# Plain float32 scores on 64 rows and plain float32 weighted values in a fused attention and MLP kernel

## The chip, the cores and the metric

One NeuronCore of one Trainium2 chip runs the whole program. The metric is the device time of one execution in microseconds. Each version is timed several times and the median counts. Hardware profiles of single executions show what each engine did.

## What is computed

Two batches, 8 heads, 576 positions, head size 64. Rotary embedding on q and k, softmax attention, then two feed-forward layers on the 1152 tokens, all in float32:

```
q_rot, k_rot = rotate(q), rotate(k)              # x1*cos - x2*sin, x1*sin + x2*cos
scores = q_rot @ k_rot.T / sqrt(64)
attn = exp(scores - max); attn /= sum(attn) + 1e-9
x = (attn @ v)  -> 1152 x 512
x = ((x @ w_a) * (x @ w_b)) @ w_out              # 512 -> 1536 -> 512
h = x @ w_in;  out = (h * tanh(softplus(h))) @ w_out2     # 512 -> 2048 -> 512
```

## The kernel before

TensorE multiplies float32 in two ways here. A tile typed `fp32r` goes through the array in one pass, and the kernel then makes a float32 product of parts: high times high, high times low, low times high. A plain float32 matmul (the parts' tile viewed as float32 by `lo32`, line 453) needs no parts; the trace shows it as two weight loads and two passes.

The kernel handles heads in pairs: p = 0 to 3 is the first batch, 4 to 7 the second. A pair's 576 queries are cut into four chunks of 128 and a rest of 64 per head. A *unit* is one chunk of one head, or both heads' rests together; nine units make a pair, 72 the attention. `UNITS` (line 442) lists them: the four chunks of head 0, the rest, the four chunks of head 1.

- **Rotation** (`rope`, line 593; called by `next_pair`, line 969, and for the first pair at line 957). Products with the tables `cs` and a sum, on VectorE or GpSimd, whichever the planner picks. Then ScalarE copies each head's 64 rows of the result into a 128-row tile, q scaled by 0.125 with its low half below (`scalar_tensor_tensor` on VectorE), k twice, and `kl` holds k's low half (line 611).
- **Scores** (`scores`, line 662). For each unit and each half of the 576 keys two `fp32r` matmuls of 288 columns on 128 rows: (q high, q low) against (k, k), and against (`kl`, 0). VectorE takes the row maximum `m`. Tag `s` has two buffers of two PSUM banks each.
- **First batch** (`attend0`, line 712). ScalarE makes E = exp(s - m) in SBUF; TensorE transposes E in 128 x 128 blocks into PSUM (`tm`, and `tr` for the last 64 keys of two heads); ScalarE copies the high half as fp16 (`ptm`, `ptr`), VectorE subtracts for the low half. V is scaled by a power of two found from its largest magnitude (`v_max`, `v_scale`) and split into two fp16 parts `vhl` (`v_split`); `vr` is its last block. The weighted values (`weighted`, line 686) are three fp16 products per block: 15 matmuls per unit, `o`. A column of ones in V gives the sum. `finish` (line 763) divides, on GpSimd for the first batch.
- **Second batch** (`attend`, line 746). E is split in place into fp16 halves `pp` and transposed by DMA; the weighted values are fp16 too.
- **Layers.** `transpose_x` brings x to `xT`. Layer 1 of the first batch uses plain float32 matmuls (tile `l` from `x`, `w`), all other layers three `fp32r` passes. Weights arrive as 64-bit words; VectorE decodes one in three operations (`xw`, `w`). The first batch's layers 1 and 2 run interleaved with the second batch's attention; then follow the second batch's layers, and the last two layers (`hidden`, `accumulate`).

Nothing is issued when it is called. `record` (line 206) collects operations, and `order` (line 289), a list scheduler with its own table of costs (`cost`, line 264) and a priority set by `at(...)`, fixes each engine's order. `any` operations go to VectorE or GpSimd, `flex` ones to ScalarE or VectorE. `OFF` shifts a unit's steps against its nominal time.

Of the kernel before, what the change touches and what calls it, by code (L numbers as in the profile page):

```python
# [20 lines left out]
NP = H // 2  # L21
# [153 lines left out]
class Plan:  # L175
# [30 lines left out]
    def record(self, engine, method, args, kw):  # L206
        key = engine.key
        out = kw["out"] if "out" in kw else args[0]
        views = [v for v in list(args) + list(kw.values()) if isinstance(v, View)]
        deps, roots = [], []  # L210
        for v in views:
            t = v.root
            assert not t.dead, t.kw
            if t.first is not None:
                deps.append((t.first, False))
            elif t not in roots:
                roots.append(t)
                deps.append((t.pool.opened, True))
                if t.before is not None:
# [44 lines left out]
    def cost(self, key, method, out, args, kw, views):  # L264
# [147 lines left out]
VM = 4  # L412
# [11 lines left out]
V_AT = 3  # L424
# [18 lines left out]
for p in range(2 * NP):  # L443
    if p == NP - 1:
        UNITS += [(p, 0, 0), (p, 0, 1), (p, 1, 0), (p, 1, 1), (p, 0, 2), (p, 0, 3), (p, None, 0), (p, 1, 2), (p, 1, 3)]
    else:
        UNITS += [(p, 0, c) for c in range(4)] + [(p, None, 0)] + [(p, 1, c) for c in range(4)]
# [10 lines left out]
def kernel(ctx: ExitStack, tc: tile.TileContext, qk, v5, w1, w2, w34, tab, out):  # L458
# [97 lines left out]
    kl = [[a_p.tile([128, S], F32R, tag=f"kl{i}{h}", name=f"kl{i}{h}") for h in range(2)] for i in range(2)]  # L556


    qz = x_p.tile([128, 2, S + 64], F32R, tag=f"x{2 * NP - 1}", name="qz")
    qz = [qz[:, i, 0:256].rearrange("p (h c) -> p h c", h=2) for i in range(2)]  # L560
    xbd = [a_p.tile([128, 128], F32, tag=f"xbd{i}", name=f"xbd{i}") for i in range(2)]
    vhl = [(a_p if i < 2 else a0_p).tile([128, 5, 2, 130], F16, tag=f"vhl{i}", name=f"vhl{i}") for i in range(3)]
# [3 lines left out]
    vr = [a0_p.tile([128, 2, 130], F16, tag=f"vr{i}", name=f"vr{i}") for i in range(3)]  # L566
    vb = (0, 1, 2, 0, 1, 0, 1, 0)
# [12 lines left out]
    def parts_tile(p):  # L580


        t = a_p.tile([128, 4, S], F32R, tag="qk", name=f"qk{p}", bufs=2)
        qk_t[p] = [(t[:, 0, :], t[:, 1, :]), (t[:, 2, :], t[:, 3, :])]
# [7 lines left out]

    def rope(p, o, k, eng, cols=slice(0, S)):

        t, raw = qk_t[p][o], qkr_t[p, o, cols.start]
        x, y = raw[:, 0, cols], raw[:, 1, cols]
        if k == 0:
            eng.tensor_tensor(x, x, cs[:, 0, cols], op=ALU.mult)
        elif k == 1:
            eng.tensor_tensor(y, y, cs[:, 1, cols], op=ALU.mult)  # L600
        elif k == 2:
            eng.tensor_tensor(x, x, y, op=ALU.add)
        else:
            for h in range(2):
                r, q = slice(64 * h, 64 * h + 64), slice(64 - 64 * h, 128 - 64 * h)
                if k == 3:
                    act.activation(t[h][r, cols], x[r], AF.Copy, scale=1.0 if o else 0.125)
                    if o:
                        act.activation(t[h][q, cols], x[r], AF.Copy, scale=1.0)
                elif o:  # L610
                    eng.tensor_tensor(kl[p % 2][h][r, cols], x[r], lo32(t[h][r, cols]), op=ALU.subtract)
                else:
                    dve.scalar_tensor_tensor(
                        t[h][q, cols], x[r], 0.125, lo32(t[h][r, cols]), op0=ALU.mult, op1=ALU.subtract
                    )
                    if cols.stop == S:
                        act.copy(qz[p % 2][:, h, r], lo32(t[h][:, 512:576]))


# [4 lines left out]
    def v_max(p):  # L624
        if p < VM:

            of = vhl[min(p, len(vhl) - 1)].rearrange("p c h e -> p (c h) e")[:, :, 1 : D + 1]
            act.activation(of, v_t[p].rearrange("p (n d) -> p n d", d=D), AF.Abs, accum_out=v_mx[:, p : p + 1])
            return
# [15 lines left out]
    def v_split(p):  # L645
# [6 lines left out]
        if p < NP:  # L652
            pool.tensor_copy(vr[vb[p]][64:128, :, 0 : 2 * D + 1], v[64:128, 4, :, 0 : 2 * D + 1])
            return
# [6 lines left out]

    def scores(n):
# [4 lines left out]
        rest = h is None  # L667
        at(t0_ + OFF["S"])
        st = s_ps.tile([128, 2, 512], F32, tag="s", name=f"s{n}")
        for hf in range(2):  # L670
            ks = slice(HS * hf, HS * hf + HS)
            ops = []
            for i in (0, 1) if rest else (h,):
                lhsT = qz[p % 2][:, i, :] if rest else tq[i][:, 128 * c : 128 * c + 128]
                ops += [(lhsT, tk[i][:, ks]), (lhsT, kl[p % 2][i][:, ks])]
            for i, (lhsT, rhs) in enumerate(ops):
                pe.matmul(st[:, hf, :HS], lhsT=lhsT, rhs=rhs, start=(i == 0), stop=(i == len(ops) - 1))

        at(t0_ + OFF["M"])
# [6 lines left out]
    def weighted(n, chunks):  # L686
# [4 lines left out]
        if rest or c % 2 == 0:  # L691
            o_t[p] = (o2_ps if o2_ps and n % 2 else o_ps).tile([128, 512], F32, tag="o", name=f"o{n}")
        o = o_t[p]
        ops = [(x, v, lo, w) for x, l, v in chunks for lo, w in ((0, D + 1), (D + 1, D)) if x is not None]
        ops += [(x, v, 0, D + 1) for l, x, v in chunks if x is not None]
        for i, (x, v, lo, w) in enumerate(ops):
# [4 lines left out]
            else:  # L701
                base = 66 * (c % 2) + oc
# [3 lines left out]
        if rest or c % 2:  # L706
            at(t_unit(n) + OFF["N"])
            finish(p, rest, h, c // 2)
# [3 lines left out]
    def attend0(n):  # L712
# [4 lines left out]
        j = 0 if rest else c % 2  # L717
# [6 lines left out]
        def parts(x, name, bufs):  # L724
# [16 lines left out]
        for i in (0,) if rest else (0, 1):  # L741
            chunks = [(*(pt_t[i][:, q, 128 * k : 128 * k + 128] for q in (0, 1)), vhl[vb[p]][:, k]) for k in range(4)]
            chunks.append((*(pr[:, q, 128 * i : 128 * i + 128] for q in (0, 1)), vr[vb[p]]))
# [19 lines left out]
    def finish(p, rest, h, g):  # L763

        key = "r" if rest else h
# [3 lines left out]
        dve.tensor_scalar(den, oo[:, :, 0], 1e-9, v_up[:, p : p + 1], op0=ALU.add, op1=ALU.mult)  # L769
# [13 lines left out]
        part = early and g  # L783
        if (p, part) not in xn_t:
# [3 lines left out]
        c = 0 if early else 2 * g  # L788
        eng.tensor_tensor(
            xn_t[p, part][:, c : c + 2, h, :], oo, den.unsqueeze(2).to_broadcast([128, 2, D]), op=ALU.mult  # L790
        )
# [133 lines left out]
    for i in range(2):  # L925
        for h in range(2):
            pool.memset(lo32(kl[i][h]), 0.0)
    parts_tile(0)
# [13 lines left out]
    v_t[0] = load_v(0, a0_p, "v", 1)  # L942
    sp.dma_start(ident, tab[:, 2 * S : 2 * S + 192])
    pool.memset(ones, 1.0)
    for i in range(2):
        pool.memset(lo32(qz[i]), 0.0)
    for i in range(2):
        pool.memset(xbd[i], 0.0)
    for i in range(3):
        pool.memset(vhl[i][:, :, :, 0:1], 1.0)  # L950
        pool.memset(vr[i][0:64], 0.0)
# [5 lines left out]
    for o, c0, c1, t in ((1, 0, KC, 0), (0, 0, QC, 0), (1, KC, S, 0), (0, QC, S, Q_REST)):  # L957
        at(t)
        for i in range(5):
            rope(0, o, i, dve, slice(c0, c1))  # L960
    at(VP[0])
    v_max(0)
    v_scale(0, 1)
    v_split(0)
    for p in range(1, NP):
        at(VP[1])
        v_t[p] = load_v(p, w_p, "raw", 3)

    def next_pair(p):
# [5 lines left out]
        parts_tile(p)  # L975
        for o in range(2):
            at(max(t0 - LOAD_LEAD, 2))
            load_qk(p, o)
            for i in range(5):
                at(t0 + dt * (R0 + R1 * (5 * o + i) / 10))  # L980
# [4 lines left out]
    for n in range(NU):  # L985
# [10 lines left out]
        if n == V_AT:  # L996
# [187 lines left out]
```

## Time and profile before

| | us |
|---|---|
| median of three runs | 621.8 |
| lowest and highest of the three | 619.88, 626.88 |
| span of the profiled execution (first to last instruction) | 619.7 |

| engine | busy us | share of the span | instructions |
|---|---|---|---|
| TensorE, matmuls (PE) | 585.8 | 95% | 4192 |
| TensorE, weight loads (PEld) | 518.4 | 84% | 4192 |
| VectorE (DVE) | 482.5 | 78% | 937 |
| ScalarE (ACT) | 305.6 | 49% | 605 |
| GpSimd (POOL) | 112.3 | 18% | 114 |

The record does not give the profiled execution a time of its own beside its span; 619.7 is 0.2 under the lowest of the timed runs and 2.1 under the median.

How to read the rows. All calculating lines carry the line number of one helper (L394), so groups are told apart by their tiles: `s<-qk` writes tile s and reads qk. In a table by stretch the columns are the stretch, its length, then for PE, PEld, DVE, ACT and POOL the busy microseconds and the number of instructions, the granted TensorE clock as a share of 2.4 GHz, the DMA share and GB/s. In a table of groups they are engine, operation, tiles, shapes and count, then busy us and mean ns of one, then idle us just before them and what ended it. A timeline row gives the start, the time to the end of the last one of the row, the engine and what it did, and the number merged. Matmuls are pipelined: one lasts some 0.2 to 0.5 us from start to end, and the distance of starts is what it costs.

### The profile page before, as it was taken

The page shows a single profiled execution, that of the slowest core. Times are in us where ns is not written, and L with a number is a line of the kernel's source. Part 1 is how long each engine was busy: PE and PEld are TensorE (multiplying, and loading weights), DVE is VectorE, ACT ScalarE, POOL GpSimd, SP SyncE. Part 2 cuts the span into 40 slices and gives each one's busy share as a digit, 9 for nine tenths or more (in the row PEclk, how much of TensorE's full clock was granted, in tenths as well). Part 3 has the DMA queues.
Part 4 walks back from the last instruction along what each step waited for, and adds up shares of the span by engine and source line. Part 5 has one row for each costly group of instructions (what it writes and reads, how often), then busy time and mean ns, then how long its engine had stood idle before and what let it go on. Part 6 is the DMA issues. An engine that isn't in the chain of part 4 may idle for free.

```text
span 619.7 us, 10977 instructions
## 1 busy us (share of the span) xinstructions
PE 585.8 (95%) x4192; PEld 518.4 (84%) x4192; DVE 482.5 (78%) x937; ACT 305.6 (49%) x605; POOL 112.3 (18%) x114
## 2 busy tenths in 40 slices
PE   5788888989989999999999999999999999999997
PEld 5677787867768778999999999997888899988985
DVE  6999998999999899896999999859989334332221
ACT  4889697556447455551444443245444344342320
POOL 5366683735152001110000000000000000000000
PEclk7799897999999999999999999999999999999999
DMA  8024131978879699799665575657887124220002
GB/s 303 2 77 128 53 116 66 264 178 205 215 181 194 151 204 211 148 184 360 214 194 183 186 228 202 237 170 259 303 285 255 52 70 153 84 68 1 1 0 86
DMA packets 78916, 100.25 MB, mean 162 GB/s; under 512 B 50832, under 2 KB 52496, under 8 KB 78864
## 3 DMA queue, kind: packets, MB, share of 16 engines
q1 hardware_dynamic: 78864, 99.55, 55.9%
q8 instruction: 33, 0.54, 0.4%
q14 instruction: 19, 0.16, 0.1%
HBM read 77.50 MB, written 10.75 MB: 142 GB/s over the span
## 4 chain that ended last, share of the span: by engine, by line
PE 71%; DVE 17%; ACT 8%; issue 2%; DMA 1%; SPq 0%; ACTq 0%; DVEq 0%
PE l L394 32%; PE acc L394 16%; PE h L394 15%; PE s L394 3%; DVE xw L394 3%; PE o L394 3%; DVE m L394 2%; ACT qk L394 2%; DVE qk L394 2%; DVE w L394 2%; DVE ptm L394 1%; ACT e L394 1%; DVE pp L394 1%; ACT ptm L394 1%; PE tm L394 1%
## 5 line engine op out<-in xcount | busy, mean ns | idle before, releaser
L394 PE MATMUL l<-x,w 128*128 128x256 f32 (+1 forms) x960 | 180.9, 343 | 0.3
L394 PEld LDWEIGHTS l<-x,w 128*128 128x128 f32 x960 | 146.1, 190 | 16.2 <-DVE ab L394 0.8
L394 DVE SCALAR_TENSOR_TENSOR xw<-wr,xw 128x512 uint32<-128x512 uint32 x184 | 131.0, 725 | 1.3
L394 PE MATMUL acc<-w,g 128*128 128x512 f32 x432 | 105.7, 396 | 0.0
L394 PE MATMUL h<-y,w 128*128 128x320 f32 (+1 forms) x576 | 104.8, 336 | 0.3 <-DVE g L394 0.3
L394 PEld LDWEIGHTS h<-y,w 128*128 128x128 f32 x576 | 93.5, 188 | 9.7 <-DVE g L394 0.7
L394 PEld LDWEIGHTS acc<-w,g 128*128 128x128 f32 x432 | 80.6, 188 | 18.5 <-ACT g L394 0.5
L394 PE MATMUL l<-ab,w 128*128 128x320 f32 (+1 forms) x576 | 79.6, 297 | 0.0
L394 PEld LDWEIGHTS l<-ab,w 128*128 128x128 f32 x576 | 77.2, 190 | 0.0
L394 DVE TENSOR_TENSOR w<-wc,w 128x512 fp32r<-128x512 f32 x39 | 26.8, 691 | 56.2 <-ACT w L394 54.8
L394 ACT CAST w<-xw 128x512 fp32r<-128x512 f32 x73 | 45.2, 622 | 43.6 <-DVE xw L394 23.1
L394 DVE TENSOR_REDUCE m<-s 128x1 f32<-128x576 f32 x72 | 53.1, 747 | 2.5 <-PE s L394 2.1
L394 ACT ACTIVATE h<-h 128x320 f32<-128x320 f32 (+1 forms) x48 | 22.8, 475 | 58.5 <-PE h L394 58.4
L394 DVE TENSOR_SCALAR xw<-wr 128x512 uint32<-128x512 uint32 x104 | 48.9, 484 | 2.9 <-DMA wr<-in_w_dram 2.4
L394 PE MATMUL s<-qk 128*128 128x288 f32 x128 | 44.3, 361 | 6.0 <-DVE qk L394 3.1
L394 DVE TENSOR_TENSOR w<-xw,w 128x512 fp32r<-128x512 f32 x66 | 45.0, 684 | 5.5 <-ACT w L394 5.3
L394 POOL TENSOR_TENSOR qkr<-qkr,cs 128x576 f32<-128x576 f32 x28 | 43.8, 1578 | 29.8 <-DMA qkr<-in_qk_dram 25.4
L394 DVE TENSOR_TENSOR g<-h,g 128x320 fp32r<-128x320 f32 (+1 forms) x48 | 26.6, 554 | 28.3 <-ACT g L394 28.3
L394 ACT CAST w<-wc 128x512 fp32r<-128x512 f32 x39 | 23.9, 617 | 38.0 <-PE acc L394 33.7
L394 ACT ACTIVATE s<-s,m 128x576 f32<-128x576 f32 x36 | 25.4, 713 | 30.8 <-DVE m L394 27.8
L394 PE MATMUL s<-kl,qk 128*128 128x288 f32 x128 | 38.1, 311 | 2.0 <-DVE kl L394 2.0
L394 PEld LDWEIGHTS s<-qk 128*128 128x128 f32 x128 | 25.3, 199 | 10.3 <-ACT e L394 4.4
(96 smaller groups left out, 753.9 us busy)
## 6 DMA issues: line engine op xcount, KB each, us to landing
wr<-in_w_dram SPq DMA_DIRECT2D x104, 512.0 KB, 4.2
wc<-kc SPq DMA_DIRECT2D x39, 256.0 KB, 2.7
kc<-xw SPq DMA_DIRECT2D x32, 256.0 KB, 2.7
qkr<-in_qk_dram SPq DMA_DIRECT2D x14, 576.0 KB, 4.9
v<-in_v_dram SPq DMA_DIRECT2D x8, 320.0 KB, 6.5
out_dram<-o_sb SPq DMA_DIRECT2D x9, 256.0 KB, 2.1
pt<-pp SPq DMA_TRANSPOSE x36, 3.7
vh<-vhl SPq DMA_DIRECT2D x8, 66.0 KB, 2.8
```

The lines of the kernel that those rows point to most:

```text
L394: getattr(engine, method)(*map(real, args), **{k: real(v) for k, v in kw.items()})
```

## The change

Three things. First, scores of both batches become plain float32: q and k keep one float32 tile per pair (`rotated`), 64 rows per head, with no halves; the factor 0.125 moves into a second set of tables `cq` for q that ScalarE makes once; `kl` and the copies by ScalarE are gone. A head's scores are one plain matmul on its 64 rows per half of the keys, head 0 on rows 0 to 63, head 1 on rows 64 to 127. The two heads of a chunk are computed together, alternating, into both score tiles, so the units are listed by chunk and not by head. The rest is a plain matmul on 128 rows. Second, in the first batch the transposed E is copied once, as float32, by ScalarE or VectorE (`flex`), and multiplied with V as float32 (`v32`), which the DMA puts into place beside the column of ones; V's scaling, splitting, `vr` and the low halves are gone there. A unit has 5 plain matmuls in place of 15 fp16 ones. Third, the planner's cost for plain matmuls changes. The second batch's weighted values stay as they are.

```diff
@@ record
-        for v in views:
+        for v in views + list(also):
...
@@ cost
+            if rhs.dtype == F32 and method == "matmul":
+                n = max(n, 560 if views[1].n == 128 else 0)
+            if rhs.a.shape[0] == 64 and rhs.dtype == F32:
+                n /= 2
...
@@ UNITS
-        UNITS += [(p, 0, c) for c in range(4)] + [(p, None, 0)] + [(p, 1, c) for c in range(4)]
+        chunks = (0, 1, None, 2, 3)
+    for c in chunks:
+        UNITS += [(p, None, 0)] if c is None else [(p, 0, c), (p, 1, c)]
...
+    def load_v32(p):
+        b, c = divmod(p, NP)
+        src = v5[b, c]
+        sp.dma_start(v32[p][:, 0:4, :, 1 : D + 1], src[:, 0:4])
+        sp.dma_start(v32[p][64:128, 4, :, 1 : D + 1], src[64:128, 4])
...
@@ rope
         elif k == 2:
-            eng.tensor_tensor(x, x, y, op=ALU.add)
-        else:
+            eng.tensor_tensor(t[:, cols], x, y, op=ALU.add)
+        elif not o and cols.stop == S:
             for h in range(2):
-                r, q = slice(64 * h, 64 * h + 64), slice(64 - 64 * h, 128 - 64 * h)
-                if k == 3:
-                    act.activation(t[h][r, cols], x[r], AF.Copy, scale=1.0 if o else 0.125)
-                    if o:
-                        act.activation(t[h][q, cols], x[r], AF.Copy, scale=1.0)
-                elif o:
-                    eng.tensor_tensor(kl[p % 2][h][r, cols], x[r], lo32(t[h][r, cols]), op=ALU.subtract)
...
+                r = slice(64 * h, 64 * h + 64)
+                act.copy(qz[p % 2][r, r], t[r, 512:576])
...
@@ scores
+        if not h:
+            at(t0_ + OFF["S"])
+            heads = (0,) if h is None else (0, 1)
+            for i in heads:
+                s_t[i] = s_ps.tile([128, 2, 512], F32, tag="s", name=f"s{n + i}")
+            for hf in range(2):
+                ks = slice(HS * hf, HS * hf + HS)
+                for i in heads:
+                    r = slice(0, 128) if h is None else slice(64 * i, 64 * i + 64)
+                    lhsT = qz[p % 2] if h is None else tq[r, 128 * c : 128 * c + 128]
+                    also = [s_t[1]] if h == hf == i == 0 else []
+                    pe.matmul(s_t[i][:, hf, :HS], lhsT=lhsT, rhs=tk[r, ks], start=True, stop=True, also=also)
...
@@ weighted
+        if p < NP:
+            ops = [(x, v, 0, D + 1) for x, v in chunks]
...
@@ attend0
-            pt = a0_p.tile([128, 2, w], F16, tag=f"p{name}", name=f"p{name}{n}", bufs=6)
-            act.copy(pt[:, 0, :], t)
-            dve.tensor_tensor(pt[:, 1, :], t, pt[:, 0, :], op=ALU.subtract)
+            pt = a0_p.tile([128, w], F32, tag=f"p{name}", name=f"p{name}{n}", bufs=6)
+            flex.copy(pt, t, scale=1.0)
...
@@ start
+        if not o:
+            act.activation(cq[:, :, c0:c1], cs[:, :, c0:c1], AF.Copy, scale=0.125)
-        for i in range(5):
+        for i in range(4):
             rope(0, o, i, dve, slice(c0, c1))
-    at(VP[0])
-    v_max(0)
-    v_scale(0, 1)
-    v_split(0)
...
```

The planner moves the work. At the start of the program, VectorE's order of before, up to the first maximum (`m`):

```order
1 L394 TENSOR_TENSOR qkr_k<-qkr_k,cs 128x320 x2
2 L394 TENSOR_TENSOR qkr_q<-qkr_q,cs 128x256
3 L394 TENSOR_TENSOR qkr_k<-qkr_k 128x320
4 L394 TENSOR_TENSOR qkr_q<-qkr_q,cs 128x256
5 L394 TENSOR_TENSOR qkr_q<-qkr_q 128x256
6 L394 TENSOR_TENSOR kl_88<-qkr_k,qk_169 64x320
...
13 L394 TENSOR_TENSOR kl_88<-qkr_k,qk_169 64x256
14 L394 TENSOR_TENSOR qkr_q<-qkr_q 128x320
15 L394 TENSOR_TENSOR kl_95<-qkr_k,qk_169 64x256
16 L394 TENSOR_REDUCE m_218<-s_192 128x1
```

And now:

```order
1 L399 TENSOR_TENSOR qkr_k<-qkr_k,cs 128x320 x2
2 L399 TENSOR_TENSOR qkr_q<-qkr_q,cq 128x256
3 L399 TENSOR_TENSOR qk_159<-qkr_k 128x320
4 L399 TENSOR_TENSOR qkr_q<-qkr_q,cq 128x256
5 L399 TENSOR_TENSOR qk_159<-qkr_q 128x256
6 L399 TENSOR_TENSOR qkr_k<-qkr_k,cs 128x256 x2
7 L399 TENSOR_TENSOR qk_159<-qkr_k 128x256
8 L399 TENSOR_TENSOR qkr_q<-qkr_q,cq 128x320 x2
9 L399 TENSOR_REDUCE m_191<-s_178 128x1
```

The four subtractions `kl` and the low halves of q are no longer there, and the products of q read `cq`.

In the middle of the first batch, TensorE's order of before holds, between the transposes `tm` and the fp16 weighted values `o` (each with its load), two units' scores from the parts in `qk` and `kl`:

```order
937 L394 MATMUL tm_1384<-ident,e_1364 128x128 x2
938 L394 MATMUL s_1389<-qk_1059 128x288
939 L394 MATMUL s_1389<-kl_108,qk_1059 128x288
940 L394 MATMUL s_1389<-qk_1059 128x288
941 L394 MATMUL s_1389<-kl_108,qk_1059 128x288
942 L394 MATMUL tm_1384<-ident,e_1364 128x128 x2
943 L394 MATMUL s_1401<-qk_1059 128x288
944 L394 MATMUL s_1401<-kl_108,qk_1059 128x288
945 L394 MATMUL s_1401<-qk_1059 128x288
946 L394 MATMUL s_1401<-kl_108,qk_1059 128x288
947 L394 LDWEIGHTS ptm_1332
948 L394 MATMUL o_1410<-vhl_143,ptm_1332 128x65
```

Now, at the same place (`s_970` is head 0, `s_971` head 1 of one chunk):

```order
160 L399 MATMUL s_970<-qk_565 128x288
161 L399 MATMUL s_971<-qk_565 128x288
162 L399 MATMUL s_970<-qk_565 128x288
163 L399 MATMUL s_971<-qk_565 128x288
164 L399 MATMUL tm_950<-ident,e_861 128x128
165 L399 MATMUL tr_979<-ident,e_861 128x128 x2
166 L399 MATMUL o_960<-v_105,ptm_916 128x65 x4
167 L399 MATMUL o_960<-v_105,ptr_921 128x65
168 L399 MATMUL tm_999<-ident,e_923 128x128 x4
169 L399 MATMUL tm_1010<-ident,e_923 128x128 x2
170 L399 MATMUL o_1015<-v_105,ptm_958 128x65 x4
171 L399 MATMUL o_1015<-v_105,ptr_990 128x65
```

The scores of a chunk stand together with the heads alternating, and ten transposes and ten weighted values stand between one chunk's scores and the next. On VectorE the same place now reads, between the maxima of two chunks, with decoding of layer-1 weights (`xw`) where subtractions stood:

```order
100 L399 TENSOR_REDUCE m_985<-s_970 128x1
101 L399 TENSOR_REDUCE m_994<-s_971 128x1
102 L399 TENSOR_SCALAR den_0_2_1003<-o_960 128x2
103 L399 TENSOR_SCALAR xw_1006<-wr_934 128x512
104 L399 RECIPROCAL den_0_2_1003<-den_0_2_1003 128x2
105 L399 TENSOR_SCALAR ptm_1017<-tm_999 128x512
106 L399 SCALAR_TENSOR_TENSOR xw_1006<-wr_934,xw_1006 128x512
107 L399 TENSOR_SCALAR xw_1031<-wr_988 128x512
108 L399 TENSOR_REDUCE m_1035<-s_1025 128x1
```

Nine of these weights are begun, and six of them finished, ahead of the first layer-1 result. In all TensorE's order has 2240 rows where it had 3430.

## Rows read from the trace of the kernel before

**Rows 1.** Table by stretch: first batch alone, interleaved (two rows), layers of second batch.
```profile
16.00:110.00 94.00, 78.02 (x900) 69.57 (x901) 88.02 (x177) 77.68 (x161) 55.06 (x56) 0.91 0.24 75
110.00:200.00 90.00, 83.26 (x574) 65.00 (x571) 88.04 (x170) 50.40 (x95) 37.47 (x26) 1.00 0.87 207
200.00:284.00 84.00, 83.89 (x709) 73.11 (x707) 77.69 (x167) 40.50 (x75) 9.41 (x7) 1.00 0.84 189
284.00:414.00 130.00, 130.00 (x972) 129.91 (x972) 115.86 (x231) 47.84 (x102) 1.42 (x4) 1.00 0.65 221
```
**Rows 2.** Groups of instructions from 16 to 110 us, VectorE and ScalarE.
```profile
L394 DVE TENSOR_REDUCE m<-s 128x1 f32<-128x576 f32 x36 | 26.6, 746 | 1.7 <-PE s L394 1.6
L394 ACT ACTIVATE e<-s,m 128x576 f32<-128x576 f32 x36 | 26.4, 744 | 5.9 <-DVE m L394 5.6
...
L394 DVE TENSOR_TENSOR ptm<-tm,ptm 128x512 f16<-128x512 f32 x36 | 24.3, 680 | 1.8 <-ACT ptm L394 1.5
...
L394 DVE SCALAR_TENSOR_TENSOR qk<-qkr,qk 64x576 fp32r<-64x576 f32 x8 | 7.8, 975 | 0.3
L394 DVE TENSOR_TENSOR ptr<-tr,ptr 128x256 f16<-128x256 f32 x16 | 6.5, 409 | 0.1
...
L394 DVE SCALAR_TENSOR_TENSOR vhl<-v,v_up,vhl 128x640 f16<-128x640 f32 x5 | 5.5, 1096 | 0.0
...
L394 DVE SCALAR_TENSOR_TENSOR xw<-wr,xw 128x512 uint32<-128x512 uint32 x4 | 3.4, 850 | 0.0
```
**Rows 3.** Chain of waits that ends last, its beginning: start us, us, what.
```profile
2.77 5.13 DMA qkr_k<-in_qk_dram
...
13.17 1.53 DVE kl L394
...
15.13 1.52 DVE kl L394
...
16.69 0.77 DVE m L394
```
**Rows 4.** Timeline of TensorE's matmuls from 61.3 to 62.4 us.
```profile
61.38 0.41 PE L394 MATMUL o<-vhl,ptm 128*128 128x65 f16 x8
61.63 0.23 PE L394 MATMUL o<-vr,ptr 128*128 128x65 f16 x2
...
61.76 0.38 PE L394 MATMUL s<-qk 128*128 128x288 f32 x1
61.97 0.30 PE L394 MATMUL s<-kl,qk 128*128 128x288 f32 x1
62.10 0.29 PE L394 MATMUL s<-qk 128*128 128x288 f32 x1
```
**Rows 5.** The same from 152 to 154.2 us: plain float32 matmuls of layer 1.
```profile
152.31 1.89 PE L394 MATMUL l<-x,w 128*128 128x256 f32 x8
154.04 0.35 PE L394 MATMUL o<-vhl,pt 128*128 128x65 f16 x6
```
**Rows 6.** Timeline of TensorE's weight loads from 85.0 to 85.8 us.
```profile
85.27 0.30 PEld L394 LDWEIGHTS xt<-ident,xbd 128*128 128x128 f32 x2
85.43 0.26 PEld L394 LDWEIGHTS tm<-ident,e 128*128 128x128 f32 x2
```
**Rows 7.** Timelines of TensorE, matmuls and weight loads, from 145.9 to 147 us.
```profile
145.67 0.81 PE L394 MATMUL l<-x,w 128*128 128x256 f32 x3
...
146.72 0.48 PE L394 MATMUL l<-x,w 128*128 128x256 f32 x1
...
146.41 0.29 PEld L394 LDWEIGHTS vs<-vm,ones 1*128 1x128 f32 x2 [0.33 <-DVE vm L394]
146.71 0.30 PEld L394 LDWEIGHTS l<-x,w 128*128 128x128 f32 x2
```
**Rows 8.** Timeline from 109.9 to 111 us: the first matmul of layer 1.
```profile
110.19 1.11 PE L394 MATMUL l<-x,w 128*128 128x256 f32 x4
```

More of the change, by code (lines that the diff above doesn't have):

```diff
@@ L218, in record @@
                 deps.append((t.pool.opened, True))
-                if t.before is not None:
+                if t.before is not None and t.before not in roots:
                     deps.append((t.before.first, False))
@@ L410 @@
 HOLD = 40
-VM = 4
 KC = 320
@@ L666, in scores @@
         tq, tk = qk_t[p]
[L667 to L677, printed above, removed]
+        if not h:
[10 more added lines that the diff above has]
+                    pe.matmul(s_t[i][:, hf, :HS], lhsT=lhsT, rhs=tk[r, ks], start=True, stop=True, also=also)
+        st = s_t[h or 0]
         at(t0_ + OFF["M"])
@@ L690, in weighted @@
         at(t_unit(n) + OFF["V"])
-        if rest or c % 2 == 0:
+        if not h:
             o_t[p] = (o2_ps if o2_ps and n % 2 else o_ps).tile([128, 512], F32, tag="o", name=f"o{n}")
         o = o_t[p]
-        ops = [(x, v, lo, w) for x, l, v in chunks for lo, w in ((0, D + 1), (D + 1, D)) if x is not None]
-        ops += [(x, v, 0, D + 1) for l, x, v in chunks if x is not None]
+        if p < NP:
+            ops = [(x, v, 0, D + 1) for x, v in chunks]
+        else:
+            ops = [(x, v, lo, w) for x, l, v in chunks for lo, w in ((0, D + 1), (D + 1, D)) if x is not None]
+            ops += [(x, v, 0, D + 1) for l, x, v in chunks if x is not None]
         for i, (x, v, lo, w) in enumerate(ops):
@@ L716, in attend0 @@
         t0_ = t_unit(n)
-        j = 0 if rest else c % 2
+        j = h or 0
         s, m = scores(n)
@@ L741, in attend0 @@
         for i in (0,) if rest else (0, 1):
-            chunks = [(*(pt_t[i][:, q, 128 * k : 128 * k + 128] for q in (0, 1)), vhl[vb[p]][:, k]) for k in range(4)]
-            chunks.append((*(pr[:, q, 128 * i : 128 * i + 128] for q in (0, 1)), vr[vb[p]]))
+            chunks = [(pt_t[i][:, 128 * k : 128 * k + 128], v32[p][:, k]) for k in range(4)]
+            chunks.append((pr[:, 128 * i : 128 * i + 128], v32[p][:, 4]))
             weighted(n if rest else n - 1 + i, chunks)
@@ L782, in finish @@
             return
-        part = early and g
+        part = early and g // 2
         if (p, part) not in xn_t:
@@ L924 @@
     pool.memset(lo32(warm), 0.0)
[L925 to L928, printed above, removed]
+    rotated(0)
     k0 = x_p.tile([128, 2, S], F32, tag="x2", name="qkr0_k")
@@ L945 @@
     for i in range(2):
-        pool.memset(lo32(qz[i]), 0.0)
+        pool.memset(qz[i], 0.0)
     for i in range(2):
         pool.memset(xbd[i], 0.0)
-    for i in range(3):
+    for i in range(NP):
+        pool.memset(v32[i][:, :, :, 0:1], 1.0)
+        pool.memset(v32[i][0:64, 4], 0.0)
+    for i in range(2):
         pool.memset(vhl[i][:, :, :, 0:1], 1.0)
-        pool.memset(vr[i][0:64], 0.0)
     at(0)
@@ L978, in next_pair @@
             load_qk(p, o)
-            for i in range(5):
-                at(t0 + dt * (R0 + R1 * (5 * o + i) / 10))
+            for i in range(4):
+                at(t0 + dt * (R0 + R1 * (4 * o + i) / 8))
                 rope(p, o, i, any_)
@@ L995 @@
         (attend0 if n < NU // 2 else attend)(n)
-        if n == V_AT:
-            at(t_unit(n) + VP[2])
-            for i in range(1, NP):
-                v_max(i)
-            v_scale(1, NP)
-            v_split(1)
-            v_split(2)
         for q, part, last, lag in XT:
@@ L1011 @@
         if u == 3 and NP - 1 <= q < 2 * NP:
+            if q < NP:
+                continue
             if q >= NP:
```

70 lines of the change are left out of this document (29 added, 41 removed).

## The prediction

> **What bounds the kernel now.** I read the busy time by stretch first [rows 1]. Four stretches matter. From the first maximum of the scores at 16.69 us [rows 3] to the first layer-1 matmul at 110.19 us [rows 8] runs the first batch's attention alone: 93.5 us, call it stage A. In it VectorE is busy for 88.0 of 94 us and TensorE for only 78.0, at a granted clock of 0.91, so some of that time is spent at 1.2 GHz and not at 2.4. From 110 to 284 us, stage B, the second batch's attention runs between the matmuls of the first batch's layers 1 and 2. There TensorE is busy for 83.3 of 90 us and then 83.9 of 84, VectorE for 88.0 and 77.7: both are nearly full, and TensorE is the one with little left to give. From 284 to 414 us TensorE has no gap, and the change touches none of that, nor of what follows.
>
> What fills VectorE in stage A is in the groups [rows 2]: 36 maxima of 746 ns, 36 subtractions `ptm` of 680 ns that make the low half of the transposed E, 16 `ptr` of 409 ns, 8 low halves of q (`qk`, 7.8 us in all) and 5 low halves of V (`vhl`, 5.5 us). So VectorE bounds stage A, and all of these but the maxima are things that the change removes.
>
> **The start.** The chain to the first maximum ends in two `kl` subtractions of 1.53 and 1.52 us on VectorE [rows 3], and both go. What is left on VectorE ahead of the first maximum are the rotations (the order of the start shows eleven, of which the last two belong to the rest of q); the products of q now wait for ScalarE's scaled tables, which it makes while the first q and k are on their way. I take 3.2 us off: the two `kl`, and a little for the low half of q, against one more wait.
>
> **Stage A, per chunk of 128 queries of both heads.** TensorE's work, from the spacing of starts at the full clock:
> - Scores before: eight passes at 0.13 us (61.97 to 62.10), and the first pass after the small fp16 matmuls starts its successor 0.21 us later, 0.08 more [rows 4]. Two units give 8 x 0.133 + 2 x 0.08 = 1.23 us.
> - Scores after: four plain float32 matmuls on 64 rows. A plain one is two passes; eight of 256 columns take 154.04 - 152.31 = 1.73 us [rows 5], 0.216 us each, so 0.243 us for 288 columns. Eight such passes one after the other are 1.94 us. No row shows two matmuls on different halves of the array. From below, the nearest row is the 0.13 us of today's single passes, 1.06 us for eight. The order of the matmuls alternates the heads, and a head's two passes stand together, so if the halves do work at once, the second pass of head 0 runs beside the first of head 1, and so on: five slots instead of eight, 1.22 us. I take this, near the lower row, since the two halves share neither rows nor score banks.
>  The Trainium skill (TensorE: Matmul & The Clock Gate, "Part 3: Packing small matmuls") states that tiles in different row groups run concurrently, with starts some 4 ns apart and strictly in order. By that it would be the five slots; no run here shows it.
> - Going to fewer rows and back: the one matmul of before on less than all rows is `vs<-vm,ones` (one row). Its two loads start at 146.41, the next load only at 146.71, 0.30 us later [rows 7], where the two loads of a full-row pair take 0.16 us, 85.27 to 85.43 [rows 6]. And the matmul behind it lasts 0.48 us, where the last of the three ahead lasts 0.81 - 2 x 0.216 = 0.38: its load is no longer hidden. The wait ahead of it is of the same kind: three matmuls spaced 0.216 from 145.67 have streamed by 146.32, and the load starts at 146.41 (the profile puts that gap down to VectorE's `vm`; the way back has no such excuse). About 0.1 us of emptying and 0.1 us of exposed load, so 0.2 us each way, 0.4 us a chunk; the bounds are 0 (a half-array might not need it) and 0.5.
>  The Trainium skill (TensorEngine Tiling (Array Packing), "Tiling Modes") says that changing the tiling mode drains the engine. The row agrees for one row against 128; with no drain the sum below would be 32 x 0.4 = 12.8 us lower.
> - Transposes: ten, about 0.11 us each, 1.1 us, as before.
> - Weighted values before: 30 fp16 matmuls, eight of which take 0.25 us (61.38 to 61.63) [rows 4], 0.93 us. After: ten plain float32 ones of 65 columns. The nearest row is `xt<-ident,xbd`, plain float32 on 64 columns: 0.16 us for its two loads [rows 6]. So 1.6 us. If every load took the 0.11 us that the first of such a pair takes, it would be 2.2 us; if the columns alone counted (0.216 x 65/256 = 0.055 a pass), 1.1 us.
>
> TensorE's sum goes from 1.23 + 1.1 + 0.93 = 3.3 to 1.22 + 0.4 + 1.1 + 1.6 = 4.3 us a chunk. VectorE and ScalarE have room: the removed groups are 24.3 + 6.5 + 7.8 + 5.5 = 44 us of VectorE's 88, while the copies of the transposed E (once, on either engine) and twelve more decoding operations of layer-1 weights come in, together some 16 us.
>
> There is a chain beside it. Both heads' score banks are written together, so the next chunk's scores wait until both exponentials have read theirs: scores 1.62, two maxima of 0.746, the second exponential 0.744 [rows 2], and handing over, some 0.4: 4.3 us. During the 2.7 us of it that are not scores TensorE has 1.1 + 1.6 us of transposes and weighted values. So two limits lie side by side, and I take 4.6 us. A rest unit: four passes 0.97, five transposes 0.55, ten passes of 130 columns 1.1: 2.7 us. Transposing x: four times 0.66. For stretches at half clock at the start, 2 us. Stage A: 16 x 4.6 + 4 x 2.7 + 2.6 + 2 = 89.0 us, 4.5 less than 93.5. VectorE's bound goes, and TensorE with the chain is late next.
>
> **Stage B.** TensorE's scores cost 1.62 - 1.23 = 0.39 us more per chunk, 16 x 0.39 = 6.2, and the four rest units (four passes 0.97 against eight 1.06 and a start) 0.2 less each: +5.4 us. Against it VectorE loses q's low halves, and the order shows nine weights begun and six finished in stage A where the trace of before has four [rows 2]: 12 operations of about 0.7 us, with the q work some 13 us that VectorE no longer does while TensorE waits for it. TensorE's own gaps there are 90 - 83.3 = 6.7 us in 110 to 200 [rows 1], and a little more inside the pipelined starts. I take 7.2 us of it back: -1.8 us in all. Removed work of ScalarE and GpSimd (`qk`, `kl`) is worth nothing in itself, they wait there.
>
> **The sum.** -3.2 - 4.5 - 1.8 = -9.5 us on the profiled 619.7 us: 610.2. The span lies 2.1 us under the median of the three runs and 0.2 under the lowest; for a median I say 610.5 us.
>
> **Rivals.**
> 1. The halves of the array do not work at once. Eight passes one after the other, 0.72 us more in each of 32 chunks, half of them in stage A, where TensorE is the limit after the change, half in stage B, where it is full: +23, 633 us. For it: no row shows an overlap. Against: disjoint rows and banks, alternating order. It decides from 1.92 us a chunk with the switches (9.5/32 = 0.3 above my 1.62): from there on nothing is won.
> 2. The switch costs nothing between half arrays, and the small plain matmuls go at their columns (1.1 us). Then TensorE needs 3.4 us and the chain 3.9; at 4.1 a chunk stage A loses 8 us more and stage B 6.4: 596 us.
> 3. The chain sets stage A: copies stand ahead of maxima and exponentials in the in-order queues of VectorE and ScalarE, or each load of the weighted values takes 0.11 us. At 5.2 us a chunk stage A is 9.6 us longer: 620 us. For it: maxima wait for scores today only 1.6 us in all [rows 2], since other work always fills in.
> 4. The change would not do what it says if the removed work were hidden anyway; VectorE's 88 of 94 us speaks against that in stage A, and it is part of 3.
>
> **Chances.** Forecast 0.53, rivals 0.13, 0.17, 0.17. One per cent, 6.2 us, is about what a measurement of this kernel tells from no change. Faster by more than that: four fifths of the forecast and all of rival 2, 0.60; the same: the rest of the forecast and most of 3, 0.22; slower: rival 1 and the tail of 3, 0.18. The range runs from rival 2 to most of the way to rival 1, 595 to 628; the forecast's own is 603 to 617.
>
> **What would show it.** Right: the first maximum at about 13.5 us; stage A near 89 us with TensorE above 90% and VectorE with gaps; starts of two scores on different halves within a few ns, a chunk's eight passes in about 1.2 us, and 0.2 us of idle loads on either side; a spacing of 0.16 us for pairs of `o`. Wrong: passes of both heads 0.24 us apart without overlap, or a stage B longer than today's 174 us.

## The result and the profile after

The changed kernel takes 614.17 us (median of four runs, 613.82 to 616.01); the kernel before took 621.38 us in the runs beside them. The ratio is 0.9884, with a 95% interval of 0.9843 to 0.9926: 7.2 us faster, 1.2%. The forecast was 610.5 us with a range of 595 to 628, so side and range hold. The profiled execution spans 612.7 us where that of before spans 619.7: 7.0 less, three quarters of the 9.5 that my sum had on the span.

The page after, engines:

```profile
PE 599.6 (98%) x3972; PEld 518.5 (85%) x3972; DVE 437.0 (71%) x872; ACT 262.7 (43%) x525; POOL 64.4 (11%) x83
```

VectorE, ScalarE and GpSimd lost 45.5, 42.9 and 47.9 us of work against the table of before. TensorE has 220 instructions fewer and is busy 14 us longer.

The table by stretch (columns as in [rows 1]; from the first maximum to the first layer-1 matmul, then from there to the last layer-1 matmul), of the kernel before:

```profile
16.69:110.19 93.50, 78.21 (x907) 69.76 (x907) 87.55 (x177) 77.58 (x160) 54.56 (x55) 0.91 0.24 75
110.19:413.31 303.12, 296.28 (x2242) 267.23 (x2238) 280.77 (x565) 138.40 (x269) 48.10 (x37) 1.00 0.77 208
```

and of the kernel after:

```profile
10.10:101.43 91.33, 88.52 (x678) 75.19 (x678) 62.52 (x128) 53.69 (x111) 44.94 (x46) 0.98 0.44 139
101.43:406.85 305.42, 301.55 (x2247) 263.25 (x2246) 266.81 (x554) 124.25 (x250) 17.38 (x17) 1.00 0.70 194
```

This is the most telling pair of the case. The first maximum comes 6.6 us earlier. Then stage A is 2.2 us shorter and stage B, taken to its last matmul, 2.3 us longer, so from the first maximum to the last layer-1 matmul the kernels need 396.6 and 396.8 us. The whole gain is the start (6.6), with some 0.5 us behind it. And in stage A the engines have changed places: VectorE is busy 62.5 of 91.3 us where it was 87.6 of 93.5, TensorE 88.5 where it was 78.2. The table that stood first [rows 1] reads for the first batch now (from 13 to 110 us):

```profile
13.00:110.00 97.00, 95.70 (x727) 81.67 (x724) 65.53 (x136) 55.92 (x116) 45.39 (x50) 0.98 0.43 132
```

The groups of VectorE from 13 to 100 us, which answer to [rows 2]:

```profile
L399 DVE TENSOR_REDUCE m<-s 128x1 f32<-128x576 f32 x34 | 24.4, 752 | 19.9 <-PE s L399 19.8
...
L399 DVE TENSOR_SCALAR ptm<-tm 128x512 f32<-128x512 f32 x5 | 3.4, 679 | 0.2 <-PE tm L399 0.2
```

Before, VectorE waited 1.6 us for scores ahead of its maxima; now it waits 19.8. This is how a bound that has moved looks: the old bottleneck stands idle behind the new one. Where 36 subtractions `ptm` stood, 5 copies are left.

**The start.** VectorE, the kernel before, from 8 us to the first maximum:

```profile
8.01 0.48 DVE L394 TENSOR_TENSOR kl<-qkr_k,qk 64x320 fp32r<-64x320 f32 x1
...
8.87 0.49 DVE L394 TENSOR_TENSOR kl<-qkr_k,qk 64x320 fp32r<-64x320 f32 x1
...
9.83 0.87 DVE L394 SCALAR_TENSOR_TENSOR qk<-qkr_q,qk 64x256 fp32r<-64x256 f32 x2
10.73 0.43 DVE L394 TENSOR_TENSOR qkr_k<-qkr_k 128x256 f32<-128x256 f32 x1
11.07 2.10 DVE L394 TENSOR_TENSOR qkr_q<-qkr_q,cs 128x320 f32<-128x320 f32 x2
13.09 1.61 DVE L394 TENSOR_TENSOR kl<-qkr_k,qk 64x256 fp32r<-64x256 f32 x1
14.63 0.47 DVE L394 TENSOR_TENSOR qkr_q<-qkr_q 128x320 f32<-128x320 f32 x1
15.13 1.52 DVE L394 TENSOR_TENSOR kl<-qkr_k,qk 64x256 fp32r<-64x256 f32 x1
```

VectorE, the kernel after:

```profile
9.15 0.89 DVE L399 TENSOR_TENSOR qkr_q<-qkr_q,cq 128x320 f32<-128x320 f32 x2
10.08 1.42 DVE L399 TENSOR_REDUCE m<-s 128x1 f32<-128x576 f32 x2
11.42 0.48 DVE L399 TENSOR_TENSOR qk<-qkr_q 128x320 f32<-128x320 f32 x1
```

The same two products of q take 2.10 us before and 0.89 after. In the kernel before, GpSimd's first rotation runs beside them, from 11.39 us; after, it begins at 12.07, and they are done by 10.04:

```profile
12.07 2.76 POOL L399 TENSOR_TENSOR qkr<-qkr,cq 128x576 f32<-128x576 f32 x2 [9.37 <-DMA qkr<-in_qk_dram]
```

**A chunk on TensorE.** Timelines of TensorE's matmuls and of its weight loads from 70 to 74 us, after:

```profile
70.07 0.72 PE L399 MATMUL o<-v,ptm 128*128 128x65 f32 x5
70.63 0.39 PE L399 MATMUL o<-v,ptr 128*128 128x65 f32 x2
70.94 1.24 PE L399 MATMUL s<-qk 64*128 64x288 f32 x8
72.12 0.66 PE L399 MATMUL tm<-ident,e 128*128 128x128 f32 x4
72.61 0.38 PE L399 MATMUL tr<-ident,e 128*128 128x128 f32 x2
72.83 1.06 PE L399 MATMUL o<-v,ptm 128*128 128x130 f32 x8
73.72 0.39 PE L399 MATMUL o<-v,ptr 128*128 128x130 f32 x2
```

```profile
70.12 0.53 PEld L399 LDWEIGHTS o<-v,ptm 128*128 128x128 f32 x4
70.57 0.30 PEld L399 LDWEIGHTS o<-v,ptr 128*128 128x128 f32 x2
70.94 0.79 PEld L399 LDWEIGHTS s<-qk 64*128 64x128 f32 x8
72.11 0.42 PEld L399 LDWEIGHTS tm<-ident,e 128*128 128x128 f32 x4 [0.38 <-issue]
```

Three things are read from starts. The weighted values: five passes from 70.07 to 70.63 and eight from 72.83 to 73.72 are both 0.112 us apart, though the first have 65 columns and the second 130; the loads go at the same pace, (70.57 - 70.12)/4 = 0.11. So a pass costs its load and not its columns, and a plain matmul, two of them, costs 0.223 us. The scores: eight passes last from 70.94 to 72.12, 1.18 us with the way back, where eight in a row at 0.242 (run 2, below) would be 1.94. The switch: the last two `ptr` passes end their turns at 70.63 + 2 x 0.112 = 70.85, and the first score and its load start together at 70.94, 0.09 later, with nothing to hide that load behind; on the way back the first transpose and its load again start together, and the load idled 0.38 us before. Start to start the switch adds up to about 0.35 us: 0.09 ahead of the scores, 1.18 - 4 x 0.242 = 0.21 in them and behind them, and 0.05 in the four transposes, which take 72.61 - 72.12 = 0.49 where four at 0.11 would be 0.44.

Whether the heads run together is seen best where only the scores are counted, in very short stretches (the stretch, its length, busy us of TensorE, number of matmuls in flight, then the clock and the DMA columns), after:

```profile
70.94:71.00 0.06, 0.06 (x2) 1.00 0.79 154
71.00:71.28 0.28, 0.28 (x2) 1.00 0.44 132
71.28:71.31 0.03, 0.03 (x4) 1.00 0.37 154
```

Two begin within the first 60 ns, none for 0.28 us, then two more within 30 ns: passes go in pairs, four slots for eight.

### The profile page after: what moved, and what is told of

Its sections match the earlier page's. It is cut to its first block, busy times and chain, and to the rows that moved or that the text cites. A ratio compares the mean times of both kernels' runs of the same rounds, so it can differ in the third digit from the quotient of the medians.

```text
span 612.7 us, 10369 instructions
## 1 busy us (share of the span) xinstructions
PE 599.6 (98%) x3972; PEld 518.5 (85%) x3972; DVE 437.0 (71%) x872; ACT 262.7 (43%) x525; POOL 64.4 (11%) x83
## 4 chain that ended last, share of the span: by engine, by line
PE 87%; DVE 5%; DMA 4%; ACT 3%; issue 2%; SPq 0%; ACTq 0%; DVEq 0%
PE l L399 35%; PE acc L399 16%; PE h L399 15%; PE o L399 8%; PE s L399 7%; PE tm L399 3%; DMA wr<-in_w_dram 2%; PE xt L399 1%; DVE m L399 1%; DMA pt<-pp 1%; DVE xw L399 1%; DMA qkr_q<-in_qk_dram 1%; DVE w L399 1%; ACT e L399 1%; PE tr L399 1%
## 5 line engine op out<-in xcount | busy, mean ns | idle before, releaser
L399 DVE SCALAR_TENSOR_TENSOR xw<-wr,xw 128x512 uint32<-128x512 uint32 x184 | 127.0, 705 | 1.6
L399 PEld LDWEIGHTS h<-y,w 128*128 128x128 f32 x576 | 93.5, 188 | 9.7 <-DVE g L399 0.7
L399 DVE TENSOR_SCALAR xw<-wr 128x512 uint32<-128x512 uint32 x104 | 47.6, 468 | 7.2 <-DMA wr<-in_w_dram 5.2
L399 DVE TENSOR_TENSOR w<-xw,w 128x512 fp32r<-128x512 f32 x68 | 46.3, 684 | 5.3 <-ACT w L399 5.1
L399 PE MATMUL s<-qk 64*128 64x288 f32 x256 | 42.4, 435 | 1.2 <-DVE qk L399 1.2
L399 ACT CAST ab<-l 128x256 fp32r<-128x256 f32 (+1 forms) x48 | 19.2, 401 | 46.4 <-DVE l L399 46.4
L399 PE MATMUL o<-v,ptm 128*128 128x65 f32 (+1 forms) x288 | 38.1, 273 | 0.5 <-ACT ob L399 0.2
L399 PEld LDWEIGHTS o<-v,ptm 128*128 128x128 f32 x288 | 35.8, 193 | 3.3 <-ACT ob L399 1.3
```

The costliest lines, as they stand in the source:

```text
L399: getattr(engine, method)(*map(real, args), **{k: real(v) for k, v in kw.items()})
```

## The experiments

Each ratio is against the kernel before, run on the same chip beside it.

**1. The order of the heads.** Theory: the overlap hangs on the alternating order. In this kernel both matmuls of head 0 are issued, then both of head 1 (in every chunk but the first).

```diff
-            for hf in range(2):
-                ks = slice(HS * hf, HS * hf + HS)
-                for i in heads:
+            for i in heads:
+                for hf in range(2):
+                    ks = slice(HS * hf, HS * hf + HS)
```

> The changed kernel, with the four score matmuls of a chunk in the order head 0, head 0, head 1, head 1 in place of alternating heads. Theory 'the halves of the array work at once': a chunk's eight passes take 0.97 us now (four pairs of starts 7 ns apart, the pairs 0.24 us apart); head by head only the meeting of the two heads can overlap, 1.45 us, or nothing, 1.94 us. TensorE is the limit of both attention stages, so 32 chunks cost 15 to 31 us more: about 630 to 645 us. Rival 'the 7 ns are only how the record shows them, the array shares its time': a chunk takes as long as before and the time stays at 614 us.

Measured: 616.75 us, ratio 0.9914 (0.9886 to 0.9942), not to be told from the changed kernel. The same short stretches, scores alone, of a chunk of this run:

```profile
63.17:63.20 0.03, 0.02 (x2) 1.00 0.73 273
63.20:63.51 0.31, 0.31 (x2) 1.00 1.00 304
63.51:63.55 0.04, 0.04 (x4) 1.00 0.74 205
```

and all eight passes in one row of its timeline:

```profile
63.18 1.25 PE L399 MATMUL s<-qk 64*128 64x288 f32 x8
```

Still two within 30 ns, then none, then two more, and 1.25 us for all, as 1.24 in the changed kernel. The rows do not name the heads. But passes of one head do not start together: once in this run head 0's two matmuls stand alone, ahead of transposes of x, and their four passes last as long as eight of both heads, where the changed kernel has one matmul of each head at that place:

```profile
98.55 1.23 PE L399 MATMUL s<-qk 64*128 64x288 f32 x4
```

```profile
97.51 0.76 PE L399 MATMUL s<-qk 64*128 64x288 f32 x4
```

So in a pair head 1's first pass must start beside head 0's first, although all four of head 0's stand ahead of it. The theory fell: the passes of the two heads run in pairs in either order of issue, and 630 to 645 us did not come. The Trainium skill (TensorE: Matmul & The Clock Gate, "Part 3: Packing small matmuls — row/col tiling") says that matmuls start in program order; taken for this kernel, that would have put head 1 behind nearly all of head 0, and these rows do not show it.

**2. All 128 rows.** Is the overlap worth time, or is it only how starts are recorded? Here each score matmul runs over all 128 rows (both heads' products are summed), so nothing can overlap and there is no switch.

```diff
...
-                    r = slice(0, 128) if h is None else slice(64 * i, 64 * i + 64)
+                    r = slice(0, 128)
```

> The changed kernel, with each score matmul on all 128 rows (each head's scores become the sum of both heads', so what is left out is the separation of the heads). No half-array matmul is left in the attention, so there is no switch, and the eight passes run one after the other: 1.94 us a chunk. Theory 'a switch costs 0.2 us each way and half arrays overlap': 1.94 against 0.97 + 0.4, 0.57 us more in each of 32 chunks, about 18 us, 632 us, and the gaps of 0.2 us ahead of and behind the scores vanish. Rival 'the gaps at the scores are waits for other engines': the gaps stay and the time is some 30 us longer, 645 us.

Measured: 628.36 us, ratio 1.0117 (1.0084 to 1.015), 14.2 us over the changed kernel, where I had expected 18. In 32 chunks that is 0.44 us each: the 0.97 us that four slots save, less some 0.5 us for the two switches. So the overlap is real, and half of what it saves goes into getting into and out of it. (Stage A ran at a granted clock of 0.98 in the changed kernel, so a little of it at 1.2 GHz, and at 1.00, all of it at 2.4 GHz, here; at an equal clock the loss would be up to 0.02 x 91.33 = 1.8 us larger, and the two switches that much cheaper, some 0.47 us.) A chunk's eight passes in the timeline of this run, with what follows at once (eight in 67.70 - 65.76 = 1.94 us, 0.242 each), and its stage A, which bears half of the loss:

```profile
65.76 2.11 PE L399 MATMUL s<-qk 128*128 128x288 f32 x8
67.70 1.00 PE L399 MATMUL o<-v,ptm 128*128 128x65 f32 x8
```

```profile
10.10:108.84 98.74, 96.88 (x680) 85.21 (x680) 61.30 (x130) 52.44 (x109) 47.56 (x47) 1.00 0.40 129
```

**3 and 4. Each half of the change alone.** In run 3 the scores are as after, and the first batch's weighted values go in fp16 halves again (V split without scaling, once per pair). In run 4 the values are as after, and the scores are those of the kernel before. A part of run 3's edit:

```diff
...
-            pt = a0_p.tile([128, w], F32, tag=f"p{name}", name=f"p{name}{n}", bufs=6)
-            flex.copy(pt, t, scale=1.0)
+                pt = a0_p.tile([128, 2, w], F16, tag=f"p{name}", name=f"p{name}{n}", bufs=6)
+                act.copy(pt[:, 0, :], t)
+                dve.tensor_tensor(pt[:, 1, :], t, pt[:, 0, :], op=ALU.subtract)
...
```

> The first part of the change alone: scores as in the changed kernel, the first batch's weighted values from fp16 halves of E and V as before (V split without a scale, from the float32 V). Theory 'TensorE bounds stage A, by the plain weighted values': TensorE's work a chunk falls by 10 x 0.223 - 0.93 = 1.3 us, but the subtractions for E's low half come back on VectorE, 24.3 + 7.6 us and 4 us for V less 7 us of copies on its 65.5 of 97 us: VectorE bounds again near 95 us of stage A, so 614 to 620 us. Rival 'the chain through both score banks sets the stage': it is unchanged, so the time stays within 2 us of 614.

> The second part of the change alone: scores from parts of q and k as before, one head after the other, and the first batch's weighted values plain float32 from V as loaded. Theory 'TensorE bounds stage A': 1.23 + 1.1 + 2.23 = 4.6 us a chunk, as with both parts (4.7), but the start does not get earlier: stage A about 92 us, stage B 2 us better than in the changed kernel at most: 616 to 621 us. Rival 'VectorE still bounds': its 88 us lose 41 us, so if it did, stage A would be far under 80 us and the time near 605 us.

Measured: run 3, the scores alone, 607.61 us, ratio 0.9793 (0.9763 to 0.9824), below the interval of the whole change; run 4, the values alone, 618.79 us, ratio 0.9965 (0.9947 to 0.9984). The scores alone win nearly twice what the whole change does, and the plain values on top of them take some 6 us back. I had expected 614 to 620 for run 3 because VectorE would be full again; it is not, and the rival's 614 did not come either. Its two stages:

```profile
9.87:96.50 86.63, 75.21 (x858) 57.79 (x859) 76.39 (x159) 60.27 (x131) 53.51 (x53) 0.98 0.45 142
96.50:398.90 302.40, 298.96 (x2248) 260.58 (x2246) 272.08 (x560) 124.55 (x251) 20.83 (x19) 1.00 0.71 198
```

VectorE and TensorE are busy for 76 and 75 of 86.6 us, and neither is full. Against the changed kernel stage A is 4.7 us shorter and stage B 3.0. The 3.0 has its rows in the groups of TensorE, from the first layer-1 matmul (101.43) to 125 us, after:

```profile
L399 PE MATMUL o<-v,ptm 128*128 128x65 f32 x16 | 2.0, 268 | 0.0
...
L399 PE MATMUL o<-v,ptm 128*128 128x130 f32 x8 | 1.1, 275 | 0.0
...
L399 PE MATMUL o<-v,ptr 128*128 128x65 f32 x4 | 0.8, 275 | 0.0
...
L399 PE MATMUL o<-v,ptr 128*128 128x130 f32 x2 | 0.4, 275 | 0.0
```

So 30 plain passes of the first batch's values are still to do when layer 1 has begun, 3.3 us at 0.112. The kernel before starts none behind its first layer-1 matmul; run 3 has 30 fp16 matmuls there, 0.9 us at 0.031 [rows 4]. That is 2.4 of the 3.0 us.

Run 4 came into its range, but not as expected: its first maximum, which I had left where it was, comes 2.5 us earlier; stage A takes 91.4 us (14.20 to 105.60), as with both parts, and stage B (to 410.3) 1.6 us more than before. So it also takes the start apart. VectorE, with the parts of q and k kept:

```profile
11.00 0.89 DVE L396 TENSOR_TENSOR qkr_q<-qkr_q,cs 128x320 f32<-128x320 f32 x2
11.80 0.41 DVE L396 TENSOR_TENSOR kl<-qkr_k,qk 64x256 fp32r<-64x256 f32 x1
12.14 0.48 DVE L396 TENSOR_TENSOR qkr_q<-qkr_q 128x320 f32<-128x320 f32 x1
12.64 1.52 DVE L396 TENSOR_TENSOR kl<-qkr_k,qk 64x256 fp32r<-64x256 f32 x1
14.20 1.42 DVE L396 TENSOR_REDUCE m<-s 128x1 f32<-128x576 f32 x2
```

```profile
12.16 4.63 POOL L396 TENSOR_TENSOR qkr<-qkr,cs 128x576 f32<-128x576 f32 x3 [7.30 <-DMA qkr<-in_qk_dram]
```

GpSimd's input lands 0.8 us later here, and the work ahead of it on VectorE is at its short durations: a `kl` of 64 x 256 takes 0.41 us before GpSimd starts and 1.52 beside it. The sum between the two `kl` (0.48) did not wait. With the same order on VectorE, that brings nearly all of the way from 16.69 to 14.20. GpSimd's first rotation starts at 11.81 to 12.61 in every run that loads V as the change does, and at 11.39 before; why the input lands later was not tried.

**5. Two key blocks less.** If TensorE bounds stage A through the loads of the values, leaving out two of the five key blocks gives their whole cost back.

```diff
-            ops = [(x, v, 0, D + 1) for x, v in chunks]
+            ops = [(x, v, 0, D + 1) for x, v in chunks[:2] + chunks[4:]]
```

> The changed kernel, with two of the five blocks of keys left out of the first batch's weighted values (transposes and copies stay). Theory 'TensorE bounds stage A, 0.223 us a plain matmul of 65 columns': 72 matmuls less, 16 us; the chain through both score banks stops it at about 4 us a chunk, so 11 to 16 us less, 598 to 603 us. Rival 'the chain sets the stage already': 612 us or more.

Measured: 608.66 us, ratio 0.9773 (0.9709 to 0.9837): 5.5 us less than the changed kernel by the medians, between the two expectations. 144 passes went, 144 x 0.112 = 16.1 us. Something else stood close behind TensorE.

**6 and 7. Without the maxima.** The nearest candidate was the chain of a chunk through both score banks. One more kernel has no maxima in the first batch (a constant bias goes to the exponential), with five blocks and with three.

```diff
...
-        dve.tensor_reduce(m, e, axis=AX.XY, op=ALU.max, negate=True)
+        if p < NP:
+            m = m0
+        else:
+            dve.tensor_reduce(m, e, axis=AX.XY, op=ALU.max, negate=True)
...
```

> The changed kernel with the first batch's row maxima left out: the exponential takes a constant bias, so no reduction stands between its score matmuls and its exponentials (the output is not the reference's). Theory: the changed kernel's stage A is held up by TensorE's own work (its intervals from matmul start to matmul start sum to about 83 of the 91 us), and the chain of a chunk through both score banks (scores, two maxima, exponentials) is only the next limit, so taking the maxima out takes just the waits away: stage A 3 to 6 us shorter, 608 to 612 us. Rival: the chain already limits the changed kernel; then a chunk gets shorter by most of its two maxima (2 x 0.75 us), stage A falls by 10 us or more, 600 to 604 us.

> The run with three key blocks (608.7 us, stage A 84 us) with the first batch's row maxima left out too (the output is not the reference's). Theory: in the run with three blocks the chain scores, maxima, exponentials through both score banks stopped the chunk at about 4.3 us; without the maxima the chain is some 1.5 us a chunk shorter and stage A comes down towards TensorE's work (some 70 us), 72 to 77 us long: 597 to 601 us. Rival: something else stopped it (ScalarE's and VectorE's copies of the transposed weights, or the rotation on GpSimd); then stage A stays at 82 to 85 us and the time at 606 to 609 us.

Measured: with five blocks 613.03 us, ratio 0.9878 (0.9819 to 0.9936), the same as the changed kernel; with three blocks 599.07 us, ratio 0.9659 (0.9591 to 0.9728), as its theory expected. From the first score matmul to the first layer-1 matmul, one table row of each kernel. After (five blocks, maxima):

```profile
8.16:101.43 93.27, 90.03 (x686) 75.79 (x686) 64.39 (x133) 53.69 (x111) 44.94 (x46) 0.98 0.45 143
```

Five blocks, no maxima:

```profile
8.38:100.60 92.22, 89.20 (x696) 75.01 (x697) 46.98 (x106) 50.90 (x107) 45.44 (x46) 1.00 0.45 145
```

Three blocks, with maxima:

```profile
8.01:94.05 86.04, 78.61 (x555) 62.55 (x555) 62.97 (x131) 50.41 (x106) 48.87 (x49) 0.98 0.49 153
```

Three blocks, no maxima:

```profile
8.00:85.22 77.22, 73.80 (x554) 59.26 (x554) 41.07 (x97) 49.74 (x105) 46.06 (x46) 1.00 0.53 170
```

Read as a square, this settles the bound. With five blocks the maxima are worth 1.1 us, with three 8.8. The two blocks are worth 7.2 us with maxima and 15.0 without, near the 16.1 of their loads. (By the medians: 1.1 and 9.6, 5.5 and 14.0. The rows with maxima are at a clock of 0.98 and those without at 1.00, so up to 1.8 us of what the maxima are worth can be the clock; the contrast is larger than that.) So the changed kernel is bound by TensorE's own work, at the full price of its loads, and some 7 us below it lies a limit that hangs on the maxima. That it is the chain of a chunk is likely, since VectorE is busy for only 63.0 of the 86.0 us with three blocks, but the maxima's place in VectorE's order was not tried apart from it. My expectation for five blocks, 3 to 6 us less, was too much: I had taken the gaps between TensorE's turns for waits; most likely they are the switches, 16 x 0.35 = 5.6 us, which stay.

**8. A mixture.** If TensorE is full with plain values and not with fp16 ones, while VectorE has room, then half of each should be better than the change: the odd chunks in fp16 halves, the even ones and the rests plain.

```diff
...
+        f16 = not rest and c % 2 == 1
...
```

> The changed kernel, with the weighted values of chunks 1 and 3 of each pair of heads in the first batch from fp16 halves, of chunks 0 and 2 and the rests plain float32. Theory 'TensorE bounds stage A and VectorE has 25 to 30% of it free': 16 units with 0.65 us less on TensorE, -10 us, while VectorE gets 16 subtractions of 0.68, 8 of 0.41 and the split of V, less some copies, and ends near 80 us in 82: 605 to 609 us. Rival 'the chain through both score banks sets the stage': 614 us, or more because VectorE's subtractions stand in front of maxima.

Measured: 606.09 us, ratio 0.9723 (0.9678 to 0.9769). It is within what its theory expected and faster than both kernels; its interval overlaps that of run 3, the scores alone. Its stage A (10.40 to 98.90 us) still has TensorE the fuller engine:

```profile
10.40:98.90 88.50, 84.56 (x758) 69.92 (x759) 73.19 (x148) 56.38 (x121) 51.62 (x50) 0.96 0.45 143
```

## Why the prediction was right, and where not

The time lies in the range in part by luck. Stages A and B together were to give 6.3 us and gave none (396.6 and 396.8 us); a start that gave twice its forecast made up for half of that.

**The start: -3.2 forecast, -6.6 measured, mis-sized.** I took the two `kl` that the chain of waits named [rows 3]. But six instructions of that kind stood ahead of the first maximum, in order on VectorE. The last two are 1.61 + 1.52 us, the two others 0.48 and 0.49, and q's two low halves 0.87, which I had set off against a wait on the tables that did not come: 4.97 us together. The sum for the rest of q went behind the maximum (0.47), and the two products run undisturbed (2.10 - 0.89 = 1.2): 6.6 in all. The last 1.2 us owes to GpSimd's start as much as to the change, as run 4 shows. With the two `kl` at the 0.41 us that one takes there, an estimate is that 2 x 1.15 + 1.2 = 3.5 of the 6.6 us are time that VectorE lost beside GpSimd.

**Stage A: -4.5 forecast, -2.2 measured.** The bound moved from VectorE to TensorE as forecast, and 4.6 us a chunk was close to TensorE's 4.7, but in part by luck. The sum of its work was 4.3; two terms in it were off, one each way, and the 0.3 on top was for a chain that does not bind here:
- Scores: five slots forecast, four measured (0.97 us and not 1.22). I let the halves run shifted by one pass, as they were issued; they start together.
- Weighted values: 0.16 us each forecast, 0.223 measured, 2.23 us a chunk and not 1.6. This is the step that failed, 10 us in 16 chunks. The lone pair [rows 6] had one of its two loads behind other work; in a run of ten there is nothing to hide behind. I had this number as the upper bound, 2.2, and chose the nearer row, though the same sum prices the rest unit's ten passes, of 130 columns, at 0.11 us each.
- The switch, 0.4 us a chunk, held: about 0.35 from the starts and 0.5 from run 2.

With these TensorE needs 0.97 + 0.4 + 1.1 + 2.23 = 4.7 us a chunk; the rest of the sum as it stood gives 16 x 4.7 + 4 x 2.7 + 2.6 + 2 = 90.6 us, against 91.3 measured. That is closer than it should be: the sum has all the values in stage A, and 3.3 us of them run behind it. Counted alike the stage is 94.6 us; of the 4 us over the sum, the table has TensorE without work for 91.33 - 88.52 = 2.8, and the rest stays open.

**Stage B: -1.8 forecast, +2.3 measured.** The forecast was +5.4 us for the scores, less 7.2 of TensorE's waits. The table has both otherwise. TensorE's time without work falls from 303.12 - 296.28 = 6.8 us to 305.42 - 301.55 = 3.9, so 3.0 came back and not 7.2: this term was mis-sized too. Its busy time grows by 5.3 us, of which 3.3 are the values left over from the first batch (run 3); they are the same mis-sized step, which I had counted in stage A. In run 3, where the rest of those values costs 0.9 us, 3.4 us of waits come back and stage B is 0.7 us shorter than before. A longer stage B was one of my signs of being wrong, and it came.

**The rivals.** The first, halves that do not overlap, is refuted by the rows of the change and by run 2. The second fell on the loads; its free switch is not seen either. Of the third, the half on loads of 0.11 us came true, which is why the result lies between the forecast and its 620; its chain is there as well, but, as far as the square shows, as the next limit and not as the bound. The fourth has something in it: VectorE's 44 us of removed work were not hidden, and still brought nothing in stages A and B together, since TensorE's new work took their place. A part of the change, the scores, does far better than the whole, and I had not priced the two halves apart.

**What stays open.** What holds run 3 at 86.6 us with no engine full; the chain through the maxima is likely, and was not tried there. Why stage B gave back less than half of the waits that I took from it.

## What to carry to other kernels

When a change moves work from a full engine to one that has room, price the new work at the rate that it has in a run of its kind, not in a lone pair where the neighbour hides half of it: short plain float32 matmuls here cost 0.112 us per load, whether 65 or 130 columns followed. Price each half of a change by itself, since the good half can pay for the bad one without anyone noticing. And when the removal of a bottleneck gives less than its size, take away the two suspected limits singly and together: only the square of four runs told which one bound and how far below it the next one lay.

## What the runs showed of the hardware

- Passes on different halves of the rows start within 30 ns of each other even when all four passes of the one half stand ahead of those of the other in the order of issue; four passes on one half alone took 1.23 us, eight on both 1.25 (run 1).
- Getting from 128 rows to 64 and back cost 0.35 us by the starts and some 0.5 by run 2; the first load on either side starts with its own matmul and has none to hide behind (70.94 and 72.12).
- A VectorE operation with two inputs took 0.41 us alone and 1.52 us beside a GpSimd product. The Trainium skill (SBUF — State Buffer, "SBUF: two separate sides") says that such an operation and a GpSimd one that reads SBUF shut each other out of a shared port for a whole instruction; the rows agree, and here that decided 2.4 us of the start.
